# Zero matmuls in TensorE's empty stretches, and low parts of probabilities on ScalarE and GpSimd, in a block-sparse attention and MLP kernel

## The chip, the cores and the metric

The kernel runs on one core of a Trainium2 chip. The metric is the device time of one execution in microseconds (us); the kernel before was timed three times: 801.17, 801.96 and 803.93, median 801.96. TensorE (PE), VectorE (DVE), ScalarE (ACT), GpSimd (POOL) and the DMA queue of SyncE (SP) each take their instructions in the order of the program and wait for each other through semaphores.

## The reference, cut to what matters

Four batches of eight heads, 768 tokens, head size 64. Queries attend in blocks of 32 tokens: each block of queries sees its neighbours, the first and the last block, and three sampled blocks; the first and the last block of queries see everything. The result, 3072 tokens by 512, goes through an MLP.

```python
attn = softmax(where(mask, q @ k.T / 8, -1e9))        # mask: window, ends, 3 sampled blocks
x = (attn @ v).transpose(0, 2, 1, 3).reshape(3072, 512)
h = x @ w_in                                          # 512 -> 2048
g = h * tanh(softplus(h))
return g @ w_out                                      # 2048 -> 512
```

The accuracy asked for is that of float32. The kernel gets it with float16 matmuls by splitting each operand into a high and a low part and taking three of the four products (high by high, high by low, low by high).

## The kernel before, in words

**Jobs.** Each batch has two dense jobs (first and last block of queries; three pieces each) and eleven jobs of two neighbouring blocks (two pieces each), in program order job 0 dense, jobs 1 to 9 pairs, job 10 dense, then more pairs. A job does, in this order: scores `s` on PE (L597, 96 matmuls for a pair), row maximum `mx` on DVE (L640), exponentials `pt` on ACT (L663), transposes `t` of the float32 probabilities on PE (L683, one per piece), the high part `ph` of each piece on ACT (L686, a cast from PSUM) and its low part `pl` on DVE (L690, one instruction that reads `t` in PSUM and `ph`), the product `o` with the values on PE (L712, 48 matmuls for a piece), the division `xs` on DVE (L731 to L734), a transpose back `tx` on PE (L741), and the two parts `xh`, `xl` of the MLP's input.

**Keys and values of a pair.** GpSimd copies the sampled blocks of keys into one of two buffers `kg` (L537, three copies for each block of queries, each with a register load), ahead of `s`. SyncE loads the sampled blocks of values from DRAM into one of two buffers `vg`: a register load and a DMA for each (L553 for the window, three at L560), ahead of `o`; a buffer is filled again only when the `o` that reads it is done.

**Weights.** `w_in` comes in eight pieces in a wide format: three DVE instructions decode each (L786, L789, L792), PE squares it (`gram_wi`, L318) for its scale, then a scaled copy `wt_i` is made on ACT, DVE or GpSimd (L840 to L844), its high part on ACT (L847) and its low part on GpSimd (L850). `w_out` goes the same way in sixteen pieces (`wor` loaded by SyncE at L778, decoded on DVE, low parts at L889); its loads wait for the decode of piece 6 of `w_in`.

**The MLP.** `h` (L928, 12 matmuls of 256 columns for half of a piece) and `y` (L987, 6 matmuls of 512 columns) are independent of the jobs once `x` of a tile of 256 tokens and the weights are there. `h` of the first tile needs jobs 0 to 4.

**The order.** A planner (class `Plan`, L85) plays the tasks through before anything is emitted: every task has an engine (or several to choose from), a cost, a key, and rings of buffers that it takes room in; of the tasks that could start, each engine takes the one with the least start and key, and the program is emitted in that order. MLP matmuls come last in choice, so they fill what the jobs leave. A table `START` (L1129) holds a time for each of the first jobs before which its scores are chosen only if PE has nothing else, `PREP` (L1104) says how many jobs ahead the next batch's tensors are prepared, `AT0`, `ATV`, `ATO`, `ATP` are keys of the preparation. `WHOLE` is the job from which the window of keys is copied by DVE too, `SPLIT` the job from which `o` of both pieces is one task. The rings: two `t`, one `o`, four `ph` and `pl`, six `raw`, three `us`.

## Time and profile before

| | |
|---|---|
| median of three runs | 801.96 us |
| the profiled execution | 802.61 us, of it 800.8 us span |
| PE busy | 731.0 us, 91% of the span |
| DVE, ACT, POOL busy | 521.2, 534.2, 350.8 us |

The page cuts the span into 40 slices of 20 us; each digit is the busy share in tenths, and PEclk is the clock granted to TensorE in tenths of full speed:

```profile
PE   4647659899999999999999999999999999999998
DVE  6998867589967755678566765895876653323230
ACT  2655335788886867887777787867786774555550
POOL 2599342489963433425433642344543431303031
PEclk9855558999999999999999999999999999999999
```

A granted clock of 5 is the lower of TensorE's two levels (1.2 GHz), 9 or more the higher (2.4 GHz). The stretch to read is the first eight slices; after them PE is full.

### The profile page before, as it was taken

The numbers are of one execution on the slowest core, as the hardware profiler recorded it, in microseconds if no ns is written. First come the engines' busy times: TensorE is split into PE (matmuls) and PEld (weight loads), VectorE is DVE, ScalarE is ACT, GpSimd is POOL, SyncE is SP. The second block draws the span as 40 slices with busy tenths as digits, with TensorE's granted clock in tenths as the row PEclk, the third lists the DMA queues.
The fourth block names the chain that finished last, engine by engine and source line by source line (L and its number), as shares of the span: only waits on it lengthen the run. The fifth ranks groups of instructions, "written<-read, shape, count | busy, mean of one in ns | idle before, by whom it ended". The sixth has DMA issues, their size and how long they took to land.

```text
span 800.8 us, 30263 instructions
## 1 busy us (share of the span) xinstructions
PE 731.0 (91%) x12626; PEld 517.2 (65%) x12626; DVE 521.2 (65%) x914; ACT 534.2 (67%) x831; POOL 350.8 (44%) x412
## 2 busy tenths in 40 slices
PE   4647659899999999999999999999999999999998
PEld 3535447767577666776677676667677676766653
DVE  6998867589967755678566765895876653323230
ACT  2655335788886867887777787867786774555550
POOL 2599342489963433425433642344543431303031
PEclk9855558999999999999999999999999999999999
DMA  7846666521424355426423455154243343000000
GB/s 283 291 156 193 199 200 181 167 76 53 138 79 137 83 158 157 117 70 213 122 55 112 124 157 163 53 169 115 65 114 98 92 127 93 14 14 14 15 14 27
DMA packets 56973, 94.23 MB, mean 118 GB/s; under 512 B 8067, under 2 KB 20356, under 8 KB 56836
## 3 DMA queue, kind: packets, MB, share of 16 engines
q1 hardware_dynamic: 56640, 92.03, 37.8%
q8 instruction: 99, 1.62, 0.9%
q14 instruction: 38, 0.31, 0.1%
q10 hardware_dynamic: 196, 0.27, 0.1%
HBM read 79.32 MB, written 12.95 MB: 115 GB/s over the span
## 4 chain that ended last, share of the span: by engine, by line
PE 73%; DVE 12%; DMA 4%; POOL 3%; issue 3%; ACT 2%; SPq 2%; POOLq 1%; ACTq 0%; DVEq 0%
PE y L987 28%; PE h L928 27%; PE t L683 5%; PE o L712 5%; PE s L597 5%; PE tx L741 1%; DMA vg<-vd 1%; DVE mx L640 1%; DVE pl L690 1%; DVE hs L961 1%; DVE us L955 1%; DVE q L445 1%; SPq L560 1%; SPq L521 1%; DMA raw_v<-in_v_dram 1%
## 5 line engine op out<-in xcount | busy, mean ns | idle before, releaser
L928 PE MATMUL h<-xh,wi 128*128 128x256 f16 x1536 | 285.0, 274 | 0.0
L987 PE MATMUL y<-wo,g 128*128 128x512 f16 x1152 | 276.6, 379 | 3.1 <-POOL wo L889 1.4
L928 PEld LDWEIGHTS <-wi 128*128 128x128 f16 x2304 | 224.8, 99 | 50.6 <-issue 1.5
L928 PE MATMUL h<-xl,wi 128*128 128x256 f16 x768 | 210.6, 274 | 0.0
L972 POOL TENSOR_TENSOR g<-hs,g 128x1024 f16<-128x1024 f32 x48 | 105.8, 2205 | 190.7 <-DVE g L969 159.9
L987 PEld LDWEIGHTS <-g 128*128 128x128 f16 x1152 | 110.4, 98 | 105.5 <-issue 6.1
L537 POOL COPY kg<-kt 128x256 f16 x264 | 119.8, 492 | 113.2 <-PE s L597 106.0
L937 ACT ACTIVATE hs<-h,gsc 128x512 f32<-128x512 f32 x96 | 65.5, 684 | 75.2 <-PE h L928 74.0
L663 ACT ACTIVATE pt<-s,nb,ns 128x256 f32<-128x256 f32 (+1 forms) x208 | 106.4, 582 | 7.6 <-DVE nb L653 3.4
L686 ACT ACTIVATE ph<-t 128x512 f16<-128x512 f32 x112 | 65.7, 595 | 56.1 <-PE t L683 38.3
L690 DVE SCALAR_TENSOR_TENSOR pl<-t,ph 128x512 f16<-128x512 f32 x112 | 75.9, 685 | 41.2 <-ACT ph L686 41.0
L683 PE MATMUL t<-ident,pt 128*128 128x128 f32 x448 | 77.9, 301 | 15.7 <-ACT pt L663 7.1
L961 DVE SCALAR_TENSOR_TENSOR hs<-us,hs 128x1024 f32<-128x1024 f32 x48 | 65.5, 1364 | 33.8 <-ACT us L960 33.8
L957 POOL TENSOR_TENSOR us<-us 128x1024 f32<-128x1024 f32 x21 | 40.9, 1947 | 79.1 <-DVE us L955 73.2
L683 PEld LDWEIGHTS t<-ident,pt 128*128 128x128 f32 x448 | 55.7, 152 | 28.2 <-DVE pl L690 8.3
L712 PEld LDWEIGHTS <-ph 128*32 128x32 f16 x3584 | 50.9, 98 | 34.3 <-issue 17.6
L955 DVE TENSOR_SCALAR us<-us 128x1024 f32<-128x1024 f32 x48 | 41.8, 870 | 39.5 <-ACT us L951 39.5
L712 PE MATMUL o<-vg,ph 128*32 128x65 f16 (+1 forms) x3072 | 52.1, 201 | 12.7 <-DMA vg<-vd 7.4
L640 DVE TENSOR_REDUCE mx<-s 128x4 f32<-128x1024 f32 x44 | 53.4, 1214 | 6.5 <-PE s L597 6.5
L951 ACT ACTIVATE us<-hs,hsc 128x1024 f32<-128x1024 f32 x48 | 55.2, 1151 | 1.0
L959 ACT ACTIVATE us<-us 128x1024 f32<-128x1024 f32 x48 | 50.6, 1055 | 4.6 <-POOL us L957 4.1
L597 PEld LDWEIGHTS <-q 64*32 64x32 f16 x2976 | 35.8, 98 | 25.4 <-issue 20.1
(190 smaller groups left out, 923.1 us busy)
## 6 DMA issues: line engine op xcount, KB each, us to landing
vg<-vd SPq DMA_DIRECT2D x304, 65.0 KB, 2.3
vg<-vd SPq DMA_DIRECT2D x80, 195.0 KB, 2.9
wr<-in_moe_w_in_dram SPq DMA_DIRECT2D x8, 1024.0 KB, 6.2
wor<-in_moe_w_out_dram SPq DMA_DIRECT2D x16, 512.0 KB, 4.9
vd<-v SPq DMA_DIRECT2D x12, 520.0 KB, 3.2
raw_k<-in_k_dram SPq DMA_DIRECT2D x12, 512.0 KB, 5.3
raw_q<-in_q_dram SPq DMA_DIRECT2D x12, 512.0 KB, 4.1
raw_v<-in_v_dram SPq DMA_DIRECT2D x12, 512.0 KB, 5.5
```

The source lines that it names most:

```text
L537: nc.gpsimd.tensor_copy(out=kgs[n][:, :, c0:c0 + BS], in_=tl["kt", b][:, :, ds(j, BS)])
L597: nc.tensor.matmul(s[g][i * BS:(i + 1) * BS, c0 + cs.start:c0 + cs.stop], q[gs, c * NPR + i, qs], src[gs, a * NPR + i, ks], start=first an ...
L663: ex = lambda o, x, g, w: nc.scalar.activation(out=o, in_=x, func=AF.Exp, bias=nb[:, g, w:w + 1], scale=tl["ns", b, sus[w]["qb"] // TB][:, ...
L683: nc.tensor.transpose(t[:, k, g], src, ident)
L686: nc.scalar.activation(out=new(sb, "ph", ("ph", i, j), [P, 2, 2, P], F16), in_=tl["t", i, j], func=AF.Copy, scale=PSC)
L690: nc.vector.scalar_tensor_tensor(out=new(sb, "pl", ("pl", i, j), [P, 2, 2, P], F16), in0=tl["t", i, j], scalar=PSC, in1=tl["ph", i, j], op ...
L712: nc.tensor.matmul(o[cs, w, g, 0:v1 - v0], p[:, k, g, cs], vt[:, k, 2 * c + g, v0:v1], start=j == 0 and g == 0 and k == 0 and n == 0, stop ...
L928: nc.tensor.matmul(h[:, f2].rearrange("p (s q) -> p s q", q=BS), wi[:, fp, w, cc, fs], x[:, :, cc], start=f2 == 0 and k == 0, stop=f2 == 1 ...
L937: nc.scalar.activation(out=tl[kq][:, 2 * (fp % 2):2 * (fp % 2) + 2], in_=tl[kh], func=AF.Copy, scale=gsc[:, fp:fp + 1])
L961: add("DVE", 1.32, lambda: nc.vector.scalar_tensor_tensor(out=hs(), in0=us(), scalar=-0.5, in1=hs(), op0=ALU.add, op1=ALU.mult), r=[ku], w ...
L972: add("POOL", 2.3, lambda: nc.gpsimd.tensor_tensor(out=g()[:, 1], in0=hs(), in1=g()[:, 0], op=ALU.subtract), r=[kq, ("gh", b, t, k)], w=[kg])
L987: nc.tensor.matmul(tl[ky], tl["g", b, t, k][:, g, f, q], wo[:, fc, w], start=fc == 0 and n == 0, stop=fc == NFC - 1 and n == 2)
```

## The change

Four things. PE gets matmuls of zeros: the planner's `fill` counts how many fit between the planned end of PE's last task and the planned start of the next, at 0.14 us each, and emits them ahead of that next task; none while the accumulation `o` of a job is between its pieces (`open`), none before 14 or after 200 us of the plan. They write columns of the PSUM bank of `o` that nothing reads; for this `o` is one fixed bank now. In the first ten jobs `pl` is no longer one DVE instruction: ACT writes the scaled piece as float32 to SBUF (`pf`, in the ring `us`), and GpSimd subtracts `ph` from it. The scaled pieces of `w_in` take their room in the ring `us` in place of `raw`. And the planner's numbers are others (`START`, `PREP` for the first batch, four keys, `WHOLE` 14, `SPLIT` 13).

```diff
-    ps = {n: ctx.enter_context(tc.tile_pool(name=f"ps_{n}", bufs=RINGS[n], space=PSUM)) for n in "stohy"}
+    ps = {n: ctx.enter_context(tc.tile_pool(name=f"ps_{n}", bufs=RINGS[n], space=PSUM)) for n in "sthy"}
+
+    obank = ctx.enter_context(tc.tile_pool(name="ps_o", bufs=1, space=PSUM)).tile([P, 512], F32, name="obank")
+    NO, NZ = 4 * (D + 2), 240
+    zeros = const.tile([P, NZ], F16, name="zeros")
+    nc.gpsimd.memset(zeros, 0.0)
...
-    WHOLE = 12
-    SPLIT = 12
+    WHOLE = 14
+    APL = 10
+    SPLIT = 13
...
+        def pf_fn(j):
+            pf = new(sb, "us", ("pf", i, j), [P, 4, TT])
+            tl["pf", i, j] = pf = pf[:, 0:2].rearrange("p f (k q) -> p f k q", k=2)
+            nc.scalar.activation(out=pf, in_=tl["t", i, j], func=AF.Copy, scale=PSC)
+
+        def plf_fn(j):
+            nc.gpsimd.tensor_tensor(out=new(sb, "pl", ("pl", i, j), [P, 2, 2, P], F16), in0=tl["pf", i, j],
+                                    in1=tl["ph", i, j], op=ALU.subtract)
...
+            if i < APL:
+
+                kf = ("pf", i, j)
+                add("ACT", 0.62, lambda j=j: pf_fn(j), r=[kj], w=[kf], new=[("us", kf)], key=-2.5)
+                add("POOL", 1.3, lambda j=j: plf_fn(j), r=[kf, ("ph", i, j)], w=[("pl", i, j)],
+                    new=[("pl", ("pl", i, j))], key=-2.5)
+                continue
...
-            t = new(sb, "raw", kt, [P, RAW], cols=NCC * 2 * P)
+            t = tl[kt] = new(sb, "us", kt, [P, 4, TT]).rearrange("p f q -> p (f q)")
...
-    AT0, ATV, ATW = -16.0, -28.0, 2.0
+    AT0, ATV, ATW = -11.0, -35.0, 2.0
...
-            PREP = (6, 4, 3) if b else (8, 1, 8)
+            PREP = (6, 4, 3) if b else (8, 3, 8)
...
-            LOADO, ATO, ATP = [("dec", 6)], -1.0, -4.0
+            LOADO, ATO, ATP = [("dec", 6)], 5.0, -6.0
...
-    RES, START = 155.0, [0, 51, 57, 72, 69, 48, 81, 72, 9, 0, 0, 0, 0, 0]
+    RES, START = 155.0, [0, 60, 93, 57, 45, 6, 69, 63, 21, 6, 51, 21, 42, 18]
...
+    def fill(a, b):
+
+        n = int((b - a - 0.15) / 0.14) if FILL[0] < a < FILL[1] and not at["open"] else 0
+        for _ in range(n):
+            nc.tensor.matmul(obank[:, NO:NO + NZ], zeros[:, 0:P], zeros, start=True, stop=True)
+        return max(n, 0)
+
+    FILL = 14.0, 200.0
+    plan.emit(pace, fill)
```

In the changed kernel the program has 235 matmuls of zeros, all ahead of the first `h`, and each with its own load of zero weights. Where they stand, and what else moved, is read from the order of the instructions. The first place is on PE, just ahead of the first `h` of the MLP. Before (`t` is a transpose of job 7, `gram_wo` a square of `w_out`):

```order
L318 LDWEIGHTS wo
L318 MATMUL gram_wo<-wo 128x128
L683 MATMUL t_1_3246<-ident,pt_2842 128x128 x4
L928 LDWEIGHTS wi
L928 MATMUL h_0_0_3281<-xh_0_1195,wi 128x256
L928 LDWEIGHTS wi
L928 MATMUL h_0_0_3281<-xl_0_1196,wi 128x256
```

And now (the rows of `obank` are the end of job 5's `o`, `t` is of job 8):

```order
L735 LDWEIGHTS pl_1_2961
L735 MATMUL obank<-vg_115,pl_1_2961 32x65
L1189 LDWEIGHTS zeros
L1189 MATMUL obank<-zeros 128x240
L691 MATMUL t_0_3520<-ident,pt_3453 128x128 x4
L951 LDWEIGHTS wi
L951 MATMUL h_0_0_3527<-xh_0_1284,wi 128x256
```

In both programs the scores of jobs 0 to 8, `o` of jobs 0 to 4 and `tx` of jobs 0 to 4 stand ahead of the first `h`; `o` of job 5 is there by one piece more now, and nine in place of ten squares of `w_out`.

The second place is on GpSimd, about the low part of the first pieces of values (`v`) and of `w_in` (`wi`). Before (`raw_q` is scaled there, `kg` are copies of keys for job 3, with their register loads between):

```order
L537 COPY kg_110<-kt_203 128x8x32
L461 TENSOR_SCALAR raw_q_1_334<-raw_q_1_334,sc_q_1_773 128x1024
L850 TENSOR_TENSOR wi<-wt_i_688,wi 128x1024
L521 TENSOR_LOAD offk
L521 ISA x2
L537 ISA
L537 COPY kg_109<-kt_203 128x8x32
```

And now:

```order
L865 TENSOR_SCALAR wt_i_721<-wi,ws_714 128x1024
L483 TENSOR_TENSOR v_0_246<-raw_v_0_154,v_0_246 128x16x64
L483 TENSOR_TENSOR v_1_250<-raw_v_1_156,v_1_250 128x16x64
L456 MEMSET v_2_846 128x16
L457 MEMSET v_2_846 128x16
L707 TENSOR_TENSOR pl_0_899<-pf_0_844,ph_0_836 128x512
L873 TENSOR_TENSOR wi<-wt_i_723,wi 128x1024
L483 TENSOR_TENSOR v_2_846<-raw_v_2_232,v_2_846 128x16x64
```

The scalings of `raw_v` and `raw_q` (L461) are gone from GpSimd here (ACT does them), a `pl` of job 1 has come in, and the last piece of values is two tasks earlier. From the end of job 1's scores to the keys of job 7 GpSimd now has 36 copies of keys, 6 `pl`, 2 scalings, 4 low parts of `v` and `q` and 4 of `wi`.

The third place is SyncE's queue, where the first gather of values (`vg`, from DRAM `vd`) begins. Before:

```order
L778 DMA wr_990<-in_moe_w_in_dram 128x4x512
L494 DMA vd_60<-v_2_942 128x2x1040
L512 DMA vg_111<-vd_60 32x1040 x2
L512 DMA vg_112<-vd_60 32x1040 x2
L553 DMA vg_111<-vd_60 64x1040
```

And now:

```order
L501 DMA vd_60<-v_2_846 128x2x1040
L801 DMA wr_1120<-in_moe_w_in_dram 128x4x512
L519 DMA vg_114<-vd_60 32x1040 x2
L519 DMA vg_115<-vd_60 32x1040 x2
L801 DMA wor_1432<-in_moe_w_out_dram 128x1024
L560 DMA vg_114<-vd_60 64x1040
```

The first load of `w_out` stands ahead of the first gather now, and the last load of `w_in` behind the last store of values.

## Rows read from the trace of the kernel before

**Rows 1.** Busy time by stretch; columns: stretch, its length, then for each engine busy us and (instructions), the granted clock, the DMA share, GB/s.
```profile
14.00:35.00 21.00, 12.70 (x210) 9.44 (x210) 20.36 (x38) 9.20 (x15) 9.08 (x17) 1.00 0.89 317
35.00:123.00 88.00, 51.89 (x1458) 39.97 (x1459) 74.29 (x128) 42.61 (x72) 61.44 (x62) 0.50 0.63 197
123.00:160.90 37.90, 34.04 (x719) 28.80 (x717) 24.37 (x60) 26.81 (x46) 12.89 (x15) 0.90 0.60 168
160.90:240.00 79.10, 75.35 (x1158) 51.91 (x1144) 69.11 (x92) 67.60 (x105) 65.97 (x58) 1.00 0.27 83
240.00:801.00 561.00, 551.02 (x9065) 382.33 (x9063) 326.58 (x571) 383.68 (x594) 199.67 (x256) 1.00 0.33 96
```
**Rows 2.** The same in slices of 20 us, the three in which DVE and then GpSimd is full.
```profile
20.00:40.00 20.00, 12.39 (x254) 10.12 (x254) 19.33 (x33) 12.62 (x19) 10.45 (x12) 0.87 0.82 291
40.00:60.00 20.00, 7.95 (x176) 6.47 (x177) 19.84 (x25) 11.88 (x16) 19.35 (x16) 0.50 0.49 156
60.00:80.00 20.00, 14.05 (x432) 10.88 (x431) 16.19 (x33) 10.19 (x20) 20.00 (x22) 0.50 0.63 192
```
**Rows 3.** The chain that ended last, pieces in order of time: start, length, what.
```profile
75.06 1.46 PE s L597 x96
...
84.04 0.78 PE o L712 x45
...
126.71 0.96 PE s L597 x88
...
128.45 1.83 issue
...
130.55 2.67 PE h L928 x12
...
137.45 1.31 PE h L928 x12
...
139.43 0.49 PE o L712 x45
...
145.08 4.75 DMA vg<-vd
```
**Rows 4.** SyncE's queue in order of time: start, length, line, what is issued and how many.
```profile
87.83 0.38 SPq L553 DMA_DIRECT2D vg<-vd  x1
...
98.08 0.38 SPq L553 DMA_DIRECT2D vg<-vd  x1
99.24 2.58 SPq L560 DMA_DIRECT2D vg<-vd  x3
...
106.37 0.37 SPq L553 DMA_DIRECT2D vg<-vd  x1
...
116.44 0.84 SPq L778 DMA_DIRECT2D wor<-in_moe_w_out_dram  x2
...
139.36 2.12 SPq L374 DMA_DIRECT2D raw_k<-in_k_dram  x3
...
154.06 0.88 SPq L553 DMA_DIRECT2D vg<-vd  x1
155.72 2.57 SPq L560 DMA_DIRECT2D vg<-vd  x3
```
**Rows 5.** GpSimd's groups of instructions between 31.5 and 81 us (all of its time there but 0.4 us): line, operation, tile, shape, count, busy us, mean ns of one, idle time before them.
```profile
L537 POOL COPY kg<-kt 128x256 f16 x30 | 18.8, 667 | 0.0
L850 POOL TENSOR_TENSOR wi<-wt_i,wi 128x1024 f16<-128x1024 f32 x6 | 15.4, 2587 | 0.1
L476 POOL TENSOR_TENSOR v<-raw_v,v 128x1024 f16<-128x1024 f32 x3 | 7.1, 2382 | 0.0
L476 POOL TENSOR_TENSOR q<-raw_q,q 128x1024 f16<-128x1024 f32 x1 | 2.6, 2571 | 0.0
```
**Rows 6.** The same columns over the whole span, the nearest operations to what GpSimd gets, and its copies of keys between 85 and 135 us.
```profile
L889 POOL TENSOR_TENSOR wo<-wt,wo 128x512 f16<-128x512 f32 x16 | 23.1, 1455 | 4.2 <-ACT wo L887 4.2
L842 POOL TENSOR_SCALAR wt_i<-wi,ws 128x1024 f32<-128x1024 f32 x2 | 2.9, 1430 | 0.6 <-DVE wo L792 0.6
...
L537 POOL COPY kg<-kt 128x256 f16 x24 | 10.6, 443 | 21.7 <-PE s L597 16.1 <-POOL kg L537 4.0 <-issue 0.9
```
**Rows 7.** Single instructions in order of time (start, length, engine, line, what, idle before): GpSimd at 113 and 154 us, DVE at 114 and 116 us, PE where the scores of job 1 end, where those of job 7 begin and at the last `o` of job 9.
```profile
32.27 0.27 PE L342 MATMUL tp_w<-wq,ones 128*128 128x2 f32 x1
...
92.28 0.28 PE L597 MATMUL s<-kt,q 64*32 64x96 f16 x8 [0.41 <-ACT pt L663]
...
160.53 0.25 PE L712 MATMUL o<-vg,ph 128*32 128x65 f16 x8
...
113.27 2.13 POOL L476 TENSOR_TENSOR q<-raw_q,q 128x1024 f16<-128x1024 f32 x1 [5.33 <-ACT q L470]
...
154.69 1.16 POOL L889 TENSOR_TENSOR wo<-wt,wo 128x512 f16<-128x512 f32 x1 [2.02 <-ACT wo L887]
...
114.01 1.67 DVE L786 TENSOR_SCALAR wo<-wor 128x512 int32<-128x512 int32 x1 [1.29 <-DMA wor<-in_moe_w_out_dram]
...
116.33 0.42 DVE L786 TENSOR_SCALAR wo<-wor 128x512 int32<-128x512 int32 x1
```
**Rows 8.** Groups of DVE and ACT between 20 and 140 us, columns as in rows 5.
```profile
L690 DVE SCALAR_TENSOR_TENSOR pl<-t,ph 128x512 f16<-128x512 f32 x19 | 13.0, 687 | 6.6 <-ACT ph L686 6.6
...
L686 ACT ACTIVATE ph<-t 128x512 f16<-128x512 f32 x20 | 11.9, 597 | 30.9 <-PE o L712 15.8 <-PE t L683 15.0
```

More of the change, by code (lines that the diff above doesn't have):

```diff
@@ L83, in room, with emit @@
         return best
-    def emit(self, pace):
+    def emit(self, pace, fill):
         for t in self.tasks:
@@ L136, in emit @@
             t.dur, fn, port = t.ways[t.eng]
+            t.fill = fill(free.get("PE", 0.0), start) if t.eng == "PE" else 0
             if port and free.get("POOL", 0.0) > start:
@@ L702, in o_fn @@
             if j == 0:
-                new(ps["o"], "o", ko, [P, 2, 2, D + 2])
+                tl[ko] = obank[:, 0:NO].rearrange("p (w g d) -> p w g d", w=2, g=2)
             o, w = tl[ko], 0 if dense else j
@@ L725, in attend @@
                 r=[k for j in js for k in (("ph", i, j), ("pl", i, j), rv(j))], w=[ko, "o in order"],
-                new=[("o", ko)] if js[0] == 0 else (), key=-3, lat=0.25, kind=("O", i))
+                new=[("o", ko)] if js[0] == 0 else (), key=-3, lat=0.25, kind=("O", i, js[-1] == nt - 1))
         def xs_fn():
@@ L844, in t_fn @@
                 nc.vector.tensor_scalar(out=t, in0=a0_i(k), scalar1=sc(), scalar2=None, op0=ALU.mult)
-        add("POOL", 1.4, lambda: t_fn("POOL"), r=[ksc, ("wi", k)], w=[kt], new=[("raw", kt)], key=cls,
+        add("POOL", 1.4, lambda: t_fn("POOL"), r=[ksc, ("wi", k)], w=[kt], new=[("us", kt)], key=cls,
             also=[("ACT", 1.16, lambda: t_fn("ACT")), ("DVE", 0.8, lambda: t_fn("DVE"))])
@@ L1127, in attn_mish_kernel @@
     total = sum(t.ways["PE"][0] for t in plan.tasks if t.kind and t.kind[0] == "M")
-    RES, START = 155.0, [0, 51, 57, 72, 69, 48, 81, 72, 9, 0, 0, 0, 0, 0]
-    at = {"done": 0.0, "next": 0.0, "job": 0, "last": None, "shape": None}
+    RES, START = 155.0, [0, 60, 93, 57, 45, 6, 69, 63, 21, 6, 51, 21, 42, 18]
+    at = {"done": 0.0, "next": 0.0, "job": 0, "last": None, "shape": None, "open": False}
     def pace(t, start):
@@ L1144, in pace @@
                     at["next"] = at["done"] + max(total - at["done"] - RES, 0.0) / max(nj - at["job"], 1)
+                elif kind == "O":
+                    at["open"] = not t.kind[2]
                 at["last"] = kind
@@ L1158, in pace @@
         return late, 0.0
-    plan.emit(pace)
+    def fill(a, b):
[5 more added lines that the diff above has]
+    plan.emit(pace, fill)
     pools["cm"].__exit__(None, None, None)
```

## The prediction

> **What bounds the kernel now.** I read the busy time by stretch first [rows 1]. From 160.9 us on PE is busy for 75.4 of 79.1 us and then for 551 of 561: there the kernel ends when PE's work ends, and a microsecond by which that state is reached earlier is a microsecond off the time. The change can win little there; what it can win lies ahead of 160.9 us, and that is where the reader should look. From 35 to 123 us PE is busy for 51.9 of 88 us and at the lower clock, so 36.1 us are empty and the 51.9 are long: the chain of waits shows scores of a pair at 1.46 us for 96 matmuls at 75 us against 0.96 us for 88 at 127, a piece of `o` at 0.78 against 0.49, a half piece of `h` at 2.67 against 1.31 [rows 3]. PE is not the bound there, though. In slices, DVE is busy for 19.3 and 19.8 of 20 us from 20 to 60 and GpSimd for 19.4 and 20.0 from 40 to 80 [rows 2]. SyncE's queue comes last: one gather of values takes 3.72 us of its time (98.08 to 99.24 + 2.58), and fourteen of them stand between 87.83 and 158.29 us, the last followed by the last `o` of job 9 at 160.53 [rows 4, 7]. So the start is passed from DVE to GpSimd to SyncE, with PE answering late, and the end of job 9 is the point at which the lead is counted.
>
> **GpSimd gets 21 subtractions and loses two scalings.** Twenty-one pieces (three of job 0, two each of nine pairs) leave DVE: 21 x 0.687 = 14.4 us [rows 8]. ACT writes 21 more casts at 0.597, 12.5 us, beside 45 us of idle time from 35 to 123 [rows 1, 8]; the scaling of three tensors comes to it too. On GpSimd no such subtraction is shown. The nearest is the low part of `w_out`, the same shape, mean 1.455 us, and 1.16 when alone [rows 6, 7]; the upper bound is the one of twice the size, 2.587 [rows 5]. I take 1.455, for GpSimd will be shared as it was in that mean. Walk GpSimd from the end of job 1's scores, 32.3 us, to the keys of job 7, by the counts of the order: 36 copies at 18.8 / 30 = 22.6; 6 `pl` 8.7; 2 scalings at 1.43, 2.9; the low parts of `v` and `q` 7.1 + 2.6; 4 of `wi` at 2.587, 10.3; 0.4 of clearing: 54.6 us, ending at 86.9 [rows 5 to 7]. Before, the scores of job 7 began at 92.28, so the lead is 5.4 us. It is won by order, since before this point GpSimd did six low parts of `wi` where four stand now, and by an earlier `v`. Bounds: copies at 0.443 and `pl` at 1.16 end it 6.6 + 1.8 us earlier; `pl` at 2.587 6.8 us later.
>
> **Zeros on PE.** 235 matmuls of 240 columns; by `h`, 12 of 256 columns in 1.31 us, one is 1.31 / 12 x 240 / 256 = 0.10 us at the higher clock and, by 2.67, 0.21 at the lower [rows 3]. In all 24 or 49 us, against 36 empty ones. Behind the waits they cost nothing; what they cost is paid where the instruction behind them was ready. 23 of them stand between the scores of job 6 and the first `o` of job 2, which frees the buffer for the next gather, so 2.3 us may be added there; I take 1.4 and carry 4.0 of the 5.4 us of lead into SyncE's queue (bounds 5.4 and 0.6, the 49 us price doubling the delay). What they give is the clock. It was low from 35 to 123 us with PE busy for 59% of the time [rows 1]; behind the first `h` scores take 0.96 us, after an empty 1.83 us at 128 a half piece of `h` takes 2.67, and at 137, with `h` close together, 1.31 [rows 3]: short empty stretches take the clock down and dense work brings it up. With 99 zeros ahead of job 1's transposes I expect it to stay up to 40 us and most of the time behind that.
>
> **SyncE's queue.** From 87.83 to 158.29 us, 70.5 us, its own work is 14 x 3.72 = 52.1, nine loads of `w_out` at 0.42 (3.8), one of `q` (0.4) and those of `k` (2.1): 58.4, so it waited 12.1 us [rows 4]. From 106.37 on, where the first `h` come between, it is 51.9 us with 42.6 of work: 9.3 us of waiting. The rows name its parts: the empty 1.83 us, `h` at 2.67 us in front of an `o`, a gather that landed 4.75 us after its issue beside the loads of `k` [rows 3]. The first load of `w_out` now stands ahead of the first gather and waits for a decode on DVE; DVE reaches that decode earlier by the seven pieces of jobs 0 to 2 that it no longer has, 4.8 us, so I put no cost on it. Of the 9.3 us PE's part goes if it answers at the higher clock; the landing stays. I take half, 4.7 (bounds 0 and 9.3).
>
> **Behind job 9.** Jobs 12 and 13 now make 96 small matmuls in place of 48 and save DVE's copies: at most the 1.05 us of a whole set each (0.96 / 88 x 96), I take 0.5 us for both. Room in `raw` for loads and earlier work on the second batch's values are hidden by PE, full there; if that cover went, the empty 3.7 us from 160.9 to 240 could grow or shrink, and I allow 2 us either way.
>
> **Sum.** -4.0 - 4.7 + 0.5 = -8.2 us on an execution of 802.6 us (800.8 of it span): 794.4. The profiled execution stands 0.65 us above the median of 801.96, so I predict 793.8 us. Its own range, from half of each term to the bounds on waits, is 788 to 799. About 0.3%, 2.4 us, is what can be told from no change.
>
> **Rivals.**
> *GpSimd becomes the bound.* It is then full from 32 to beyond 100 us. For it: 21 x 1.455 = 30.6 us more in a stretch with 26.6 us empty (88 - 61.4) [rows 1]. Against: nearly all of that room lay behind 81 us, where the walk has ended. With `pl` at 2.587 the lead at job 7 is gone, and only the 4.7 us and less remain: 797 to 801, centre 799.
>
> *DVE is held up by GpSimd's subtractions* (the slower end). At 114.01 us a DVE step on `w_out` took 1.67 us while GpSimd ran 113.27 to 115.40; two steps later the same took 0.42 [rows 7]. If each new subtraction holds DVE for its length, 30.6 us are added and 14.4 removed, 16 us; the later half falls into DVE's idle 13.7 us from 35 to 123 [rows 1], the first half, 8, into the stretch where it is full [rows 2]. The lead of 4.0 becomes a loss of 4, and the waits stay: 802.6 + 4 + 0.5, some 806.5 at the median. It decides from the point where more than half of the subtractions hit a decode. The old `pl` read PSUM and was outside that quarrel, which is for it; against it, GpSimd was full from 40 to 80 us before, so decodes there met it already.
> The Trainium skill, "SBUF — State Buffer", section "SBUF: two separate sides", states it as a rule: VectorE with two SBUF inputs or in a two-port mode and GpSimd take one shared pair of ports as an exclusive lock, and the second waits for the whole instruction of the first. The single instruction above agrees with it; by the rule alone, with every subtraction meeting a decode, the time would be the 806.5 of this rival.
>
> *The clock is not held.* The zeros were counted from planned gaps, none between the pieces of `o`; where PE is later than planned they run out and it stands empty. Then they cost 0.21 us each where late, the lead at SyncE falls to 0.6 and the 9.3 us stay: 801.9.
>
> *Everything answers at once.* The clock is high throughout and SyncE never waits: -5.4 - 9.3 + 0.5, or 787.8 and, with the copies at 0.443, down to 781: centre 785.
>
> **Chances.** Forecast 0.48; clock and queue better 0.14; GpSimd bound 0.14; clock not held 0.10; DVE held up 0.14. Faster by over 0.3% (below 799.6): 0.48 + 0.14 + 0.10 of the third = 0.72. Within 0.3%: 0.04 of the third and 0.07 of the fourth and 0.01 of the fifth, 0.12. Slower: 0.03 + 0.13 = 0.16. The range 784 to 805 leaves out the end of the best case and most of the slower one.
>
> **What would show it.** Right: the granted clock from 35 to 123 us above 0.75; scores of job 7 near 87 us; the first gather behind `o` of job 2 at 85; the last `o` of job 9 near 152 in place of 160.5; the stretch behind it as long as before. Wrong: `pl` on GpSimd over 2 us each, GpSimd without a gap past 110 us; DVE's decodes longer than before with DVE full to 100 us; a clock at 0.50 with zeros of 0.21 us in front of instructions that were ready; or a lead at job 9 that PE does not keep to the end.

## The result, and the profile after

The changed kernel takes 809.24 us in the median (806.71 to 811.46) where the kernel before, run beside it, takes 801.96 (797.28 to 803.93): ratio 1.0091, 95% interval 1.0064 to 1.0118. It is slower by 0.9%. All medians here leave out one execution of the run e15 below, which took 1238 us at a granted clock of 0.56. The forecast was 793.8 us and the range ended at 805, so direction and range were both wrong.

The profiled execution took 807.37 us, 805.6 of it span. Its slices of 20 us, each digit the busy share in tenths:

```profile
PE   5866678798999999999999999999999999999998
...
DVE  5996997688887575678675765796776653324230
...
POOL 2699876589764454434543441453553531203031
PEclk9978868999999999999999999999999999999999
```

The clock did what was hoped: 7, 8, 8, 6 in the slices from 40 to 120 us where a 5 stood before. GpSimd is fuller from 80 to 140 us (8, 7, 6 for 3, 4, 2). The busy time by stretch, columns as in [rows 1]:

```profile
14.00:35.00 21.00, 17.16 (x275) 13.93 (x276) 18.41 (x30) 7.65 (x14) 12.29 (x18) 1.00 0.86 312
35.00:123.00 88.00, 61.42 (x1570) 48.84 (x1568) 78.30 (x118) 51.09 (x88) 79.21 (x75) 0.77 0.59 187
123.00:160.90 37.90, 32.35 (x695) 26.67 (x696) 27.95 (x51) 25.01 (x47) 20.80 (x18) 0.86 0.63 189
160.90:240.00 79.10, 73.16 (x1168) 51.36 (x1166) 66.32 (x96) 63.39 (x96) 62.68 (x55) 0.98 0.33 102
```

Against [rows 1] PE is busy for 61.42 us in place of 51.89 from 35 to 123, at a granted clock of 0.77 in place of 0.50, but that holds 27 us of zeros. DVE, which should have lost 14.4 us of work over the first ten jobs, is busier there, 78.30 against 74.29. GpSimd went from 61.44 to 79.21. And the two stretches behind, where PE should have been full, lost: 32.35 against 34.04, and 73.16 against 75.35.

**The first place where the changed kernel falls behind** is PE between the scores of job 4, which begin at 65.64 us (67.45 before), and those of job 5, at 78.02 (74.99 before). Rows are start, length, engine, line, what, idle before:

```profile
71.42 0.28 PE L605 MATMUL s<-kt,q 64*32 64x96 f16 x8 [4.89 <-POOL q L483]
71.48 0.35 PE L605 MATMUL s<-kg,q 64*32 64x160 f16 x8
71.77 4.81 PE L1189 MATMUL obank<-zeros 128*128 128x240 f16 x26
76.41 0.62 PE L325 MATMUL gram_wi<-wi 128*128 128x128 bf16 x8
```

PE waits 4.89 us for the low part of the second piece of queries, which on GpSimd now stands behind copies of keys and two subtractions. When it comes, 4.8 us of zeros stand next in line: the planner saw a gap here, the chip had its gap earlier, and the zeros are pure delay for the squares behind them.

**DVE got its 14.4 us back as stretched decodes.** DVE's three decode steps of `w_out` between 20 and 140 us (line, operation, tile, shape, count, busy us, mean ns, idle), before:

```profile
L789 DVE SCALAR_TENSOR_TENSOR wo<-wor,wo 128x512 int32<-128x512 int32 x16 | 11.4, 720 | 0.0
...
L792 DVE SCALAR_TENSOR_TENSOR wo<-wor,wo 128x512 int32<-128x512 int32 x14 | 10.3, 742 | 0.0
L786 DVE TENSOR_SCALAR wo<-wor 128x512 int32<-128x512 int32 x16 | 8.8, 560 | 1.3 <-DMA wor<-in_moe_w_out_dram 1.3
```

and after:

```profile
L815 DVE SCALAR_TENSOR_TENSOR wo<-wor,wo 128x512 int32<-128x512 int32 x13 | 16.6, 1274 | 0.0
L812 DVE SCALAR_TENSOR_TENSOR wo<-wor,wo 128x512 int32<-128x512 int32 x15 | 14.9, 999 | 0.0
L809 DVE TENSOR_SCALAR wo<-wor 128x512 int32<-128x512 int32 x16 | 14.3, 902 | 0.0
```

30.5 us for 46 instructions became 45.8 us for 44. Besides, DVE took over three high parts of `w_in` from ACT, 4.1 us. One stretch shows how the decodes grew; DVE's and GpSimd's timelines side by side:

```profile
90.68 0.62 DVE L809 TENSOR_SCALAR wo<-wor 128x512 int32<-128x512 int32 x1
91.22 2.62 DVE L815 SCALAR_TENSOR_TENSOR wo<-wor,wo 128x512 int32<-128x512 int32 x1
93.76 2.35 DVE L809 TENSOR_SCALAR wo<-wor 128x512 int32<-128x512 int32 x1
96.03 1.64 DVE L812 SCALAR_TENSOR_TENSOR wo<-wor,wo 128x512 int32<-128x512 int32 x1
```

```profile
90.99 4.83 POOL L873 TENSOR_TENSOR wi<-wt_i,wi 128x1024 f16<-128x1024 f32 x2
95.79 1.33 POOL L707 TENSOR_TENSOR pl<-pf,ph 128x512 f16<-128x512 f32 x1
```

Three decodes in a row end at 93.84, 96.11 and 97.67 us, 0.3 to 0.6 us behind the end of a GpSimd instruction each (about 93.4, 95.82, 97.12): each lasts until the instruction of GpSimd that began before it is done, and then a little less than it takes alone (0.42 to 0.68 us). Note that two of the three meet a low part of `w_in`, not a new subtraction. The low parts of `w_in` come later now and meet the decodes of `w_out`; the decodes of `w_in` did not get shorter by it, 33.8 us for 23 between 20 and 140 us against 32.7 before. The Trainium skill, "SBUF — State Buffer", section "SBUF: two separate sides", has a rule for the ports that VectorE and GpSimd share: an exclusive lock for a whole instruction, against VectorE with two SBUF inputs or in a two-port mode. The trace agrees for the first and the third decode, which read two tensors; for the second, which reads one, it shows the wait but not the mode.

### The profile page after: what moved, and what is told of

The parts are those of the page before. It is cut to its first block, busy times and chain, and to the rows that moved or that the text cites. A ratio compares the mean times of both kernels' runs of the same rounds, so it can differ in the third digit from the quotient of the medians.

```text
span 805.6 us, 30860 instructions
## 1 busy us (share of the span) xinstructions
PE 748.8 (93%) x12909; PEld 532.9 (66%) x12909; DVE 530.3 (66%) x897; ACT 539.3 (67%) x844; POOL 386.2 (48%) x436
## 4 chain that ended last, share of the span: by engine, by line
PE 73%; DVE 10%; DMA 5%; POOL 3%; issue 3%; SPq 3%; ACT 2%; POOLq 1%; ACTq 0%; DVEq 0%
PE y L1010 29%; PE h L951 26%; PE obank L735 5%; PE t L691 5%; PE s L605 5%; DMA vg<-vd 2%; PE obank L1189 1%; PE tx L764 1%; DVE wo L815 1%; SPq L528 1%; DVE wt L907 1%; DVE wo L812 1%; POOL kg L544 1%; SPq L567 1%; DVE wo L809 1%
## 5 line engine op out<-in xcount | busy, mean ns | idle before, releaser
L995 POOL TENSOR_TENSOR g<-hs,g 128x1024 f16<-128x1024 f32 x48 | 103.6, 2158 | 187.5 <-DVE g L992 146.8
L544 POOL COPY kg<-kt 128x256 f16 x264 | 121.8, 501 | 101.0 <-PE s L605 95.5
L960 ACT ACTIVATE hs<-h,gsc 128x512 f32<-128x512 f32 x96 | 65.6, 683 | 85.2 <-PE h L951 84.1
L698 DVE SCALAR_TENSOR_TENSOR pl<-t,ph 128x512 f16<-128x512 f32 x91 | 61.8, 684 | 34.1 <-ACT ph L694 33.9
L980 POOL TENSOR_TENSOR us<-us 128x1024 f32<-128x1024 f32 x25 | 48.3, 1930 | 70.8 <-DVE us L978 69.6
L691 PE MATMUL t<-ident,pt 128*128 128x128 f32 x448 | 72.9, 286 | 4.8 <-DVE pl L698 3.2
L978 DVE TENSOR_SCALAR us<-us 128x1024 f32<-128x1024 f32 x48 | 37.6, 782 | 49.1 <-ACT us L974 49.1
L691 PEld LDWEIGHTS t<-ident,pt 128*128 128x128 f32 x448 | 52.7, 145 | 17.5 <-issue 3.6
L735 PE MATMUL obank<-vg,ph 128*32 128x65 f16 (+1 forms) x3072 | 50.7, 199 | 9.0 <-DMA vg<-vd 6.4
L982 ACT ACTIVATE us<-us 128x1024 f32<-128x1024 f32 x48 | 50.7, 1057 | 5.5 <-POOL us L980 5.0
L983 ACT ACTIVATE us<-us 128x1024 f32<-128x1024 f32 x48 | 50.6, 1055 | 0.7
```

What stands on the lines that cost most here:

```text
L544: nc.gpsimd.tensor_copy(out=kgs[n][:, :, c0:c0 + BS], in_=tl["kt", b][:, :, ds(j, BS)])
L691: nc.tensor.transpose(t[:, k, g], src, ident)
L698: nc.vector.scalar_tensor_tensor(out=new(sb, "pl", ("pl", i, j), [P, 2, 2, P], F16), in0=tl["t", i, j], scalar=PSC, in1=tl["ph", i, j], op ...
L735: nc.tensor.matmul(o[cs, w, g, 0:v1 - v0], p[:, k, g, cs], vt[:, k, 2 * c + g, v0:v1], start=j == 0 and g == 0 and k == 0 and n == 0, stop ...
L960: nc.scalar.activation(out=tl[kq][:, 2 * (fp % 2):2 * (fp % 2) + 2], in_=tl[kh], func=AF.Copy, scale=gsc[:, fp:fp + 1])
L995: add("POOL", 2.3, lambda: nc.gpsimd.tensor_tensor(out=g()[:, 1], in0=hs(), in1=g()[:, 0], op=ALU.subtract), r=[kq, ("gh", b, t, k)], w=[kg])
```

## The experiments

Names used below: *zeros*, *subtractions* (on GpSimd), *numbers* (the planner's other numbers and the ring for the scaled pieces of `w_in`). Every ratio is to the kernel before on the same chip, whose median lay between 800.0 and 801.3 us in these runs. "Piece" counts the pieces of `o` in order on PE: three of job 0, two of each further job, so that piece 21 is the last `o` of job 9. A trace is one execution, and executions of one kernel differ: the twelve of e1 go from 800.0 to 810.9 us.

### One part at a time

**e1**, the changed kernel without zeros, in its order.

```diff
-    FILL = 14.0, 200.0
+    FILL = 0.0, 0.0
```

> The changed kernel without its 235 zero matmuls, every other instruction in its place. Theory Z (the zeros cost: 28 of them take 71.8 to 76.6 us in front of matmuls that were ready, and 6.4 us are waits of zeros on the division xs, since they write the bank that xs reads): 4 to 8 us less than the changed kernel's 809.2, so 801 to 805, the granted clock from 35 to 123 us back at 0.50 to 0.60. Theory G (the subtractions on GpSimd cost: DVE's decodes of w_out last 1.54 us in place of 0.76, the low part of the second piece of queries comes at 71 us): within 2 us of 809.2, or later if the clock was worth something. Theory N (the planner's other numbers cost): the same as G, 807 to 812.

Measured 804.58 us, ratio 1.0046 (1.0020 to 1.0072): 0.45%, some 4 us less than the changed kernel and still slower than before. Theory Z is right in part: the zeros cost, and something else does too.

**e2**, the kernel before with zeros alone: the order of before on every engine, with 231 zeros in it. As a change of the changed kernel (`AT0`, `ATV`, `PREP`, `ATO`, `ATP` and the ring go back likewise):

```diff
-    WHOLE = 14
-    APL = 10
-    SPLIT = 13
+    WHOLE = 12
+    APL = 0
+    SPLIT = 12
...
-    RES, START = 155.0, [0, 60, 93, 57, 45, 6, 69, 63, 21, 6, 51, 21, 42, 18]
+    RES, START = 155.0, [0, 51, 57, 72, 69, 48, 81, 72, 9, 0, 0, 0, 0, 0]
```

> The kernel before, instruction by instruction, with the zero matmuls that the same rule counts, on the fixed bank. Theory Z: slower than before by 3 to 8 us (805 to 810), with zeros waiting for xs in the trace. Theories G and N: the zeros raise the clock and cost little, 798 to 803; the clock from 35 to 123 us at 0.7 or more.

Measured 793.48 us, ratio 0.9920 (0.9898 to 0.9942). Against theory Z, the zeros alone make the kernel 7.4 us faster than 800.87. This is the fastest version found.

```profile
35.00:123.00 88.00, 60.23 (x1610) 48.60 (x1609) 78.75 (x132) 43.95 (x78) 61.91 (x63) 0.76 0.64 202
123.00:160.90 37.90, 35.74 (x746) 29.86 (x745) 27.62 (x63) 29.99 (x51) 17.27 (x16) 0.98 0.63 180
160.90:240.00 79.10, 75.55 (x1272) 52.17 (x1270) 69.58 (x95) 67.76 (x105) 61.80 (x57) 1.00 0.28 86
```

In its windows the clock is 0.76 from 35 to 123 us, as in the changed kernel, and PE is fuller behind, not emptier.

**e3**, the changed kernel without subtractions, and **e10**, the same without zeros (`FILL = 0.0, 0.0`): the numbers with and without zeros.

```diff
-    APL = 10
+    APL = 0
```

> The changed kernel with the low parts of the first ten jobs on VectorE again, as before (the order is planned anew). Theory G: 4 to 8 us less than 809.2, 801 to 805, and the decodes of w_out between 35 and 123 us back near 0.8 to 1.0 us. Theory Z: within 3 us of 809.2. Theory N: within 3 us of 809.2, since the numbers stay.

> The changed kernel with the planner's new numbers and the ring, without zeros and with the low parts on VectorE (run e3 without its zeros, the same order but for them). If the numbers alone are bad: above 820, 826 to 830 with a gain of 7 us by the zeros of e3, 815 to 819 with a loss of 4 by them. If it is the zeros that hurt these numbers: 800 to 806.

Measured 820.96 (ratio 1.0239, 1.0212 to 1.0265) and 817.73 (1.0209, 1.0174 to 1.0243). The numbers alone lose 16 us. Not early: in e10 the scores of job 7 begin at 84.1 us (92.28 before) and piece 21 ends at 156.9 (161.1). They lose behind it:

```profile
160.90:240.00 79.10, 67.36 (x923) 44.49 (x921) 61.50 (x86) 59.41 (x95) 58.98 (x48) 0.94 0.26 79
```

PE is busy for 67.36 us there in place of 75.35 [rows 1].

**e4**, the subtractions alone, and **e9**, the same with zeros. Against e2, and in e4 with `FILL = 0.0, 0.0` besides:

```diff
-    APL = 0
+    APL = 10
```

> The kernel before, with its numbers, its ring and no zeros, but with the low parts of the first ten jobs by ScalarE and GpSimd (the order is planned anew). Theory G: 806 to 812, decodes of w_out between 35 and 123 us longer than 1.2 us on average. Theories Z and N: 799 to 804.

> The kernel before with its numbers and its ring, with the subtractions on GpSimd and with zeros (run e4 plus zeros, the same order but for them). If zeros act by themselves as on the kernel before (7.4 us less): 810 to 813. If they cost wherever the subtractions make PE's planned gaps wrong (as in the changed kernel, 4.6 us more than without): 821 to 825.

Measured 818.81 (1.0218, 1.0196 to 1.0240) and 822.58 (1.0267, 1.0240 to 1.0294). The subtractions alone lose 18 us; the zeros add 4 there. PE in e4 at the scores of jobs 4 and 5:

```profile
71.61 0.28 PE L605 MATMUL s<-kt,q 64*32 64x96 f16 x8 [4.71 <-POOL q L483]
76.06 0.28 PE L605 MATMUL s<-kt,q 64*32 64x96 f16 x8 [4.04 <-ACT pt L671]
78.51 0.34 PE L605 MATMUL s<-kg,q 64*32 64x160 f16 x8 [1.53 <-POOL kg L544]
```

Of the three waits the first and the last are GpSimd's.

So the parts don't add up. As ratios: zeros 0.992; subtractions 1.022; numbers 1.021; zeros and subtractions 1.027; zeros and numbers 1.024; subtractions and numbers 1.005 (e1); all three 1.009. Subtractions and numbers lose 18 and 16 us alone, and together 4: these numbers suit this set of subtractions and not the kernel before. The zeros gain in the order of before alone.

**e5**, the changed kernel's order with the subtractions done by DVE, at the places where GpSimd's stood.

```diff
         def pf_fn(j):
-            pf = new(sb, "us", ("pf", i, j), [P, 4, TT])
...
+            pass
+
+        plf_fn = pl_fn
```

> The changed kernel in its own order on every engine, zeros included, but each of the 21 subtractions is done by VectorE from PSUM, as before, at the place where GpSimd's stood; ScalarE's casts to float32 are left out. This asks what the subtractions on GpSimd cost where nothing else is planned anew. Theory G (they cost, by GpSimd's time and by holding up VectorE's decodes): 798 to 805 against 809.2, the low part of the second piece of queries done by 66 us, decodes of w_out below 1.2 us on average between 35 and 123. Theory N (the order itself costs): 808 to 815, since VectorE has 14.4 us more to do.

Measured 815.52, ratio 1.0172 (1.0137 to 1.0207), 6 us slower than with GpSimd. Theory G falls in this form: in this order the subtractions are better on GpSimd, stretched decodes and all.

### Where the subtractions cost

**e13** and **e14**, run e4 with the subtractions of jobs 0 to 3 alone (9, `APL = 4`) and of jobs 5 to 9 alone (10, the edit below).

```diff
-            if i < APL:
+            if 5 <= i < APL:
```

> Run e4 (the kernel before with subtractions on GpSimd, 818.8) with those of jobs 0 to 3 alone, 9 of 21 (the order is planned anew). If the price is GpSimd's full stretch from 40 to 80 us, where they delay the low part of the queries and the copies of keys: 811 to 819. If it is the later ones, which hold up VectorE's decodes of w_out: 800 to 806.

> The same with the subtractions of jobs 5 to 9 alone, 10 of 21. GpSimd full from 40 to 80 us as the place: 799 to 804. Decodes of w_out as the place: 808 to 818.

Measured 811.35 (1.0127, 1.0092 to 1.0162) and 800.94 (1.0000, 0.9973 to 1.0028). The first nine cost 11 us. The later ten cost nothing, though they are the ones that meet the decodes of `w_out`, which took 39.9 us for 48 in e14 against 30.5 for 46 before. So the larger part of the price in the order of before comes from the subtractions in GpSimd's full stretch [rows 2], and the decodes of `w_out`, as far as they were held in e14 (0.83 us each; 0.66 before, 1.04 in the changed kernel), are hidden. From 35 to 123 us PE in e13 waits 4.7 us for the low part of the second piece of queries, none before, and 17.3 us for gathers, 5.4 before; the decodes of `w_in` took 34.2 us for 23 against 32.7, so they can be a small part only. The two runs leave out the two subtractions of job 4, and the 18 us of e4 are 7 more than both together: those 7 us are not accounted for.

**e6**, the changed kernel with the second piece of queries first in choice.

```diff
-                parts(b, "q", j, 4)
+                parts(b, "q", j, 4 if (b, j) != (0, 1) else -30)
```

> The changed kernel with one key altered: the preparation of the second piece of batch 0's queries comes first in choice (key -30 in place of 4; the order is planned anew). If the wait of 4.9 us at 71.4 us reaches the end of the kernel: the last 16 matmuls of job 4's scores without a wait and 803 to 806. If it is covered by later waits, or something else is late in its place: 807 to 812.

Measured 820.55 (1.0226, 1.0188 to 1.0264). The wait of 4.89 us went (the scores of job 4 wait 0.66 us, for a copy of keys), and the kernel is 11 us slower: the new order from there on loses more than the wait cost. A wait seen in a chain is no price as long as removing it changes the plan behind it.

### What the zeros do

**e7** and **e8**, the changed kernel and e2, each without the zeros between the last piece of an `o` and the transpose back, where a zero waits for `xs` because both use one bank (6.4 us in four waits in the changed kernel).

```diff
+                    at["xs"] = True
+                elif kind == "X":
+                    at["xs"] = False
...
-        n = int((b - a - 0.15) / 0.14) if FILL[0] < a < FILL[1] and not at["open"] else 0
+        n = int((b - a - 0.15) / 0.14) if FILL[0] < a < FILL[1] and not at["open"] and not at["xs"] else 0
```

> The changed kernel in its own order without those 35 zeros that stand between the last piece of an o and the transpose back of its job, where the next matmul of zeros waits for the division xs that reads the same bank. If the waits of the zeros on xs (6.4 us from 35 to 140 us) delay the matmuls behind them: 803 to 806. If PE would have waited there anyway: 807 to 811.

> The kernel before with zeros, without those 69 of 231 that stand between the last piece of an o and the transpose back of its job. If these delay work: 789 to 792. If they hold the clock: 794 to 799. With the 231 the time was 793.5.

Measured 810.81 (1.0104, 1.0066 to 1.0143) and 799.69 (0.9978, 0.9949 to 1.0007). In the changed kernel those zeros cost nothing: PE would have waited for `xs` anyway. In e2 they carry nearly the whole gain.

**e15**, the changed kernel with the zeros ahead of 40 us alone (`FILL = 14.0, 40.0`); **e17**, with half of the zeros in every gap.

```diff
-        n = int((b - a - 0.15) / 0.14) if FILL[0] < a < FILL[1] and not at["open"] else 0
+        n = int((b - a - 0.15) / 0.28) if FILL[0] < a < FILL[1] and not at["open"] else 0
```

> The changed kernel with the 99 zeros planned ahead of 40 us alone, every other instruction in its place. Without zeros it took 804.6, with all 235 809.2; the first 20 us of zeros put the scores of job 1 1.4 us later and the first o 1.9. If that early delay is carried to the end: 806 to 808. If the cost comes from the later zeros (28 of them ahead of the squares at 72 us): 803 to 805.5. If the early zeros start the clock up and it is kept: 800 to 803.

> The changed kernel with half of the zeros in every gap, 112, every other instruction in its place. If blocks longer than the real gaps are what costs: 800 to 804 (some clock, no delay; without zeros 804.6). If in this order a higher clock gives nothing, since other engines set the pace: 804.5 to 807. If zeros cost by their number: 806.5 to 807.5.

Measured 804.90 (1.0059, 1.0035 to 1.0082) and 804.33 (1.0051, 1.0025 to 1.0078): both as e1, without zeros. In the profiled execution of e17 the clock is the same as with all zeros:

```profile
35.00:123.00 88.00, 56.33 (x1668) 42.94 (x1672) 79.30 (x120) 53.07 (x96) 84.00 (x76) 0.77 0.64 200
```

So the net cost of some 4 us is not in the zeros ahead of 40 us and not in the first half of each block; what is left is the second half of the later blocks, time by which they are longer than the real gaps. Whether the higher clock, 0.77 against 0.61 in e1, is worth anything in this order is not shown: that execution of e17 took 799.71 us, not the median of 804.33, and the twelve fall into two groups by the granted clock of the whole span, five at 0.966 to 0.969 with 798.2 to 803.9 us and seven at 0.955 to 0.959 with 803.1 to 809.1.

**e16** and **e18**, e2 with the same line at 0.11 us a zero (295 zeros) and at 0.17 (188).

> Run e2 (the kernel before with 231 zeros, 793.5) with each planned gap filled at 0.11 us a zero in place of 0.14, 295 zeros. If the clock is what pays and still falls in the gaps: 789 to 793. If the zeros are longer than the gaps by now: 795 to 800.

> The kernel before with the planned gaps filled at 0.17 us a zero, 188 zeros in place of 231 (793.5). If shorter blocks keep the clock and delay less: 790 to 793.5. If the clock is lost in the rest of the gap, as with the 162 of run e8 (799.7): 796 to 800.

Measured 805.10 (1.0070, 1.0044 to 1.0095) and 800.25 (1.0000, 0.9982 to 1.0019). 231 zeros gain 7 us, 188 and 162 gain nothing to speak of, 295 lose 5. The clock alone doesn't explain it: from 35 to 123 us it is 0.76 in e2 and 0.76 in e18, and 0.82 in e16, the slowest of the three. PE's own matmuls do get shorter. Without the zeros PE is busy for 731.0 us in the kernel before, 705.5 in e2, 707.3 in e18 and 705.6 in e16, some 24 to 26 us less each time. But the rest of the span, empty or spent on zeros, grows from 69.8 us to 83.9, 88.7 and 97.2: most of what the clock gives comes back as waiting, and the three differ in how much. In the changed order it is the same, 728.7 and 73.5 us in e1, 712.1 and 93.5 with all zeros.

The difference is there by the time SyncE's queue reaches the loads of the next batch's keys (`raw_k`), which stand behind the fourteenth gather in the order of before and behind the fifteenth in the changed one. The trace columns belong to the profiled execution, whose own time stands beside them:

| | loads of keys issued | piece 21 ends | this execution | median |
|---|---|---|---|---|
| before | 139.4 | 161.1 | 802.6 | 800 to 802 |
| e2, 231 zeros | 136.2 | 156.0 | 791.2 | 793.5 |
| e18, 188 | 138.9 | 160.0 | 797.8 | 800.3 |
| e8, 162 | 139.5 | 161.2 | 801.6 | 799.7 |
| e16, 295 | 144.3 | 165.3 | 804.5 | 805.1 |
| e17, changed, 112 | 139.2 | 158.7 | 799.7 | 804.3 |
| e1, changed, 0 | 139.9 | 159.7 | 804.0 | 804.6 |
| e15, changed, 99 | 142.2 | 160.9 | 803.9 | 804.9 |
| changed, 235 | 145.1 | 163.4 | 807.4 | 809.2 |

Within one order the time of the execution follows this column, but for 0.1 us between e1 and e15. It is a place on the way and not a cause: it says that the difference arises ahead of it and is kept. Why 231 zeros bring SyncE there 3 us earlier and 188 half a microsecond isn't settled; that the gain depends on how the lengths of the blocks fall against the gathers is a guess.

### The landing beside the keys

Without zeros (e1) piece 18 ends 8.6 us earlier than before (141.7 against 150.3) and piece 19 only 2.1 earlier (151.4 against 153.4). That is not a lead of 8.6 us lost. At the end of piece 18 the kernel before has done 120 matmuls of `h` and e1 84; the 36 are 3.9 us at 1.31 us for 12 [rows 3], and 24 of them come between the two pieces in e1. And the kernel before has its own wait for a gather behind it by then. Before:

```profile
149.38 0.25 PE L712 MATMUL o<-vg,ph 128*32 128x65 f16 x8 [1.81 <-DMA vg<-vd]
```

Of the 6.5 us by which e1 takes longer from piece 18 to piece 19, 2.6 are those 24 matmuls and 2.4 a longer wait; the rest are squares of `w_out` and transposes that stand behind piece 18 there. PE, and SyncE's queue ahead of it, in e1:

```profile
150.56 0.25 PE L735 MATMUL obank<-vg,ph 128*32 128x65 f16 x8 [4.16 <-DMA vg<-vd]
```

```profile
139.91 1.50 SPq L381 DMA_DIRECT2D raw_k<-in_k_dram  x3
141.50 0.55 SPq L560 DMA_DIRECT2D vg<-vd  x1
142.83 3.04 SPq L567 DMA_DIRECT2D vg<-vd  x3
```

**e11** and **e12** issue these loads two gathers later, in e1 and in e2; nothing else moves.

```diff
+        if (what, b) == ("k", 1):
+            load_k = fn
+            fn = lambda: held.append([2, load_k])
         add("SP", 0.5 * n, fn, r=after, w=keys,
...
                 nc.sync.dma_start(out=vg[p0:p0 + BS, c0 // P], in_=vd[b][ds(j, BS)])
+            for h in held:
+                h[0] -= 1
+                if not h[0]:
+                    h[1]()
```

> Run e1 (the changed kernel without zeros) with the three loads of the next batch's keys, 1.5 MB, issued two gathers later on SyncE; nothing else moves. In e1 the eighteenth piece of o ended 8.6 us earlier than before (141.7 against 150.3 us) and the nineteenth waited 4.2 us for a gather that landed beside these loads. If that landing loses the lead: the nineteenth piece at 147 or earlier and 800 to 802 against 804.6. If PE has too little to do there and waits elsewhere: 803.5 to 806.

> Run e2 (the kernel before with zeros alone, 793.5) with the same loads two gathers later. If the landings beside them cost there too: 789 to 792; if they are hidden: 792.5 to 795; if the keys of the next batch then come late: 795 to 799.

Measured 806.76 (1.0065, 1.0041 to 1.0089) and 798.71 (0.9967, 0.9946 to 0.9988). In e11 the wait in front of piece 19 is gone: 5.2 us lie between the ends of pieces 18 and 19, against 9.6 in e1, and pieces 19 and 20 end at 148.95 and 153.34, 2.4 and 2.9 us earlier than in e1. Then ACT, in its fixed order, waits for the late keys, and PE for ACT:

```profile
153.40 1.06 ACT L316 ACTIVATE I-4162_4163<-raw_k 128x1024 f16<-128x1024 f32 x1 [5.79 <-DMA raw_k<-in_k_dram]
```

```profile
157.42 0.37 PE L960 MATMUL h<-xh,wi 128*128 128x256 f16 x1 [3.71 <-ACT hs L969]
```

ACT waits 5.79 us for the keys that it is to square, the scaled copy of `h` (`hs`) comes behind it, and the next `h` has no room. One wait of 4.16 us became another of 3.71. In e12 it is the same: ACT waits 5.45 us for the keys, PE 2.62 us for `hs`, and of the 7 us that the zeros of e2 had gained 5 are gone. The runs show that the gather waits beside these loads and doesn't without them; they don't show what the kernel would be with keys that land without harm, since those reading them weren't moved.

## Why the prediction was wrong

The order of e1 and of the changed kernel is one, so the terms can be read in both and the zeros as the difference. The steps are those of the sum; negative is earlier than before, in us, and the sums are those of the spans (802.2 and 805.6 against 800.8):

| step | forecast | e1, no zeros | changed |
|---|---|---|---|
| lead carried to SyncE's first gather behind `o` of job 2, 87.83 before | -4.0 | -0.9 (86.90) | +3.4 (91.23) |
| the fourteen gathers, 70.5 us before | -4.7 | -2.4 (68.1) | -2.5 (68.0) |
| from there to the end of job 9's last `o`, 2.8 us before | 0 | +1.9 (4.7) | +1.4 (4.2) |
| behind job 9, to the end of job 13's `o`, 82.5 us before | +0.5 | +3.8 (86.3) | +2.8 (85.3) |
| the rest, 557.2 us before | 0 | -1.0 (556.2) | -0.3 (556.9) |
| sum | -8.2 | +1.4 | +4.8 |

These are single executions. e1 and e11 are one program up to 139 us, and the end of piece 15 differs by 2.7 us between them (130.61 and 133.27): a term of one or two us can be chance. The first row isn't: the piece of `o` for which that gather waits begins at 85.5 to 86.5 us in e1, e11, e15 and e17, at 90.55 in the changed kernel, and at 83.97 before.

**GpSimd gets 21 subtractions.** The walk over GpSimd was right: in e1 the keys of job 7 are ready at 87.23 us for the 86.9 forecast, and its scores begin 4.5 us earlier than before, with a subtraction at 1.55 us in the mean (32.3 us for 21 between 20 and 140 us) for the 1.455 taken. It took a low part of the queries as a term of the sum, though, and not as something for which job 4 waits, 4.11 us in e1. **The step that failed is the next one**, "carry 4.0 of the 5.4 us of lead into SyncE's queue". SyncE's gather doesn't wait for scores. It waits for two other things, and in e1 both end at 86.43 us. One is the first `o` of job 2, which reads the buffer. In the changed order scores run ahead of `o`: when job 2's second piece of `o` ends, 720 score matmuls are done in e1 and 624 before, and the piece itself ends at 90.54 us against 89.81. The other is a load of `w_out` just ahead of the gather, which waits 2.9 us for a decode on DVE (2.8 in the changed kernel, 2.9 to 3.5 in e11, e15 and e17; before, no wait of SyncE in this place was over 0.3). Of the first load of this kind the prediction had said "I put no cost on it".

Before: job 2's first `o`; the scores of job 7 and the gather are in [rows 7] and [rows 4].

```profile
83.97 0.30 PE L712 MATMUL o<-vg,ph 128*32 128x65 f16 x8
```

e1: job 2's first `o`, the scores of job 7, the decode, the load of `w_out`, the first and the last of the fourteen gathers. Then the same in the changed kernel.

```profile
85.59 0.30 PE L735 MATMUL obank<-vg,ph 128*32 128x65 f16 x8
...
87.77 0.28 PE L605 MATMUL s<-kt,q 64*32 64x96 f16 x8 [0.68 <-ACT pt L671]
...
85.55 0.88 DVE L815 SCALAR_TENSOR_TENSOR wo<-wor,wo 128x512 int32<-128x512 int32 x1
...
86.45 0.36 SPq L801 DMA_DIRECT2D wor<-in_moe_w_out_dram  x1
86.90 1.87 SPq L560 DMA_DIRECT2D vg<-vd  x1
...
152.43 2.55 SPq L567 DMA_DIRECT2D vg<-vd  x3
```

```profile
90.55 0.25 PE L735 MATMUL obank<-vg,ph 128*32 128x65 f16 x8
...
91.67 0.23 PE L605 MATMUL s<-kt,q 64*32 64x96 f16 x8 [0.23 <-ACT pt L671]
...
89.88 0.87 DVE L815 SCALAR_TENSOR_TENSOR wo<-wor,wo 128x512 int32<-128x512 int32 x1
...
90.78 0.36 SPq L801 DMA_DIRECT2D wor<-in_moe_w_out_dram  x1
91.23 0.39 SPq L560 DMA_DIRECT2D vg<-vd  x1
...
156.65 2.55 SPq L567 DMA_DIRECT2D vg<-vd  x3
```

So of 4.5 us of lead at the scores 0.9 reach SyncE without zeros, and with them it starts 3.4 us late. Which of the two, `o` or the decode, would hold the gather alone was not separated, nor what makes them late; in e1 the transposes just ahead of that `o` wait 1.85 us for a step of DVE as well.

**SyncE's queue.** "Of the 9.3 us PE's part goes ... the landing stays. I take half, 4.7." Half of that came, 2.4 and 2.5 over the fourteen gathers. The landing didn't stay as it was: the loads of `k` stand one gather later in SyncE's queue and are issued at 139.91 us in e1, as before at 139.36 [rows 4], and PE's wait for a gather beside them was 4.16 us in place of 1.81, and 2.80 in the changed kernel. (A gather takes 3.74 us by the rows quoted, for the 3.72 used; nothing hangs on it.)

**The end of job 9** was "the point at which the lead is counted". It doesn't serve between two orders. By the end of job 9's last `o` PE has done 180 matmuls of `h` before, and 156 of `h` and six of `y` in e1 and the changed kernel: 2.6 us of `h` put off for 1.5 us of `y`. The 1.4 us by which e1 stands earlier there is mostly work put off.

**Behind job 9.** "Jobs 12 and 13 ... I take 0.5 us for both ... I allow 2 us either way." It was 3.8 in e1 and 2.8 in the changed kernel, of which 1.0 and 0.3 came back in the rest. Job 13 is the next batch's first dense job, so only job 12 changed: 3024 score matmuls for 2976. The largest single wait there is a transpose of a job whose low part has stayed on DVE. In the changed kernel:

```profile
194.03 0.66 PE L691 MATMUL t<-ident,pt 128*128 128x128 f32 x4 [3.17 <-DVE pl L698]
```

The same wait was 0.82 us before, and PE's clock in this stretch, 1.00 in [rows 1], was 0.98. Which of the numbers did it was not separated; e10 shows that they can cost far more here.

**Zeros on PE.** The price of one was right: 36.7 us for 235, 0.156 each, between the 0.10 and 0.21 of the two levels. What failed as well is the size of the delay, "behind the waits they cost nothing ... I take 1.4": at the start of the scores of job 7 they cost 3.9 us (91.67 against 87.77), at SyncE's first gather 4.3, at the end of job 13's `o` 2.6, in the median 4. The clock rose as forecast, above 0.75, and PE's own matmuls took 712.1 us for 728.7 in e1, but the rest of the span grew by 20.0: the prediction's own first paragraph said that PE was not the bound there, and then counted PE's answers as if it were.

**The rivals.** "DVE is held up by GpSimd's subtractions" named the right mechanism: 14.4 us off DVE, 15 or more back in the decodes of `w_out`. Its 806.5 came near the 809.2, but that this was the reason is not shown, nor is it excluded: in e14 decodes of `w_out` that were held less cost nothing, and in e1 SyncE's load ahead of the first gather and the transposes ahead of job 2's `o` wait for DVE. "The clock is not held" was wrong, the clock was held. That the zeros alone would give 793.5, almost the forecast, is a coincidence of numbers.

**The signs that were named.** Clock above 0.75: yes, 0.77. Scores of job 7 near 87: in e1 alone. First gather behind `o` of job 2 at 85 (83.8 by the 4.0 of the sum): 91.23. Last `o` of job 9 near 152: its last piece begins at 162.83 us, 160.53 before [rows 7]. Stretch behind as long as before: no.

## What to carry to other kernels

Count a lead on the instruction for which the next queue waits: scores 4.5 us early gave SyncE 0.9, since it waits for `o` and, at a load in front of it, for a decode. Between two orders, count at each point the work that fills in as well: 36 matmuls of `h` put off look like 3.9 us of lead. Order numbers, and which engine does a piece of work, belong together: each alone cost 16 to 18 us here and both 4, so a part's price can't be read from a kernel planned for another. Filling matmuls are worth trying alone, with two or three lengths: the same idea gave -7, 0 and +5 us by how long the blocks were, at clocks of 0.76, 0.76 and 0.82.

## What was not expected of the hardware

A decode on DVE that began behind a GpSimd instruction ended 0.3 to 0.6 us behind the end of that instruction, 2.62, 2.35 and 1.64 us in a row for 0.42 to 0.68 alone, even where the decode reads a single tensor (the step of line 809). And a higher granted clock did not order the times: from 35 to 123 us it was 0.76, 0.76 and 0.82 in executions of 791.2, 797.8 and 804.5 us (e2, e18, e16), with PE's own matmuls at 705.5 to 707.3 us in all three.
